# Where VectorE's sums of a weight matrix stand in a fused attention and ELU kernel: program order, halves, and the order of four copies

## Chip, cores, metric

One core of a Trainium2 chip. The metric is the device time of one execution in microseconds (us). The program runs on one core.

## The reference, cut to what matters

```python
x = attn(x, state)          # (8 batches, 544 tokens, 512): token rows and state rows
h = x @ w_in                # 4352 x 512 @ 512 x 2048
g = where(h > 0, h, exp(min(h, 0)) - 1)
out = g @ w_out             # 4352 x 2048 @ 2048 x 512, fp32
```

The kernel works batch by batch. Per batch there is a first product (**FFN1**: 16 rows of h, transposed, 128 x 512 each, two matmuls a row, which a trace shows as four records, then ELU) and a second product. Batch 0 forms the second product plainly, while the weights are still arriving. From batch 1 on it is a seven-product (Strassen) scheme, which needs sums of quarters of w_out; VectorE forms these once, about the time when batch 1 begins.

## The kernel before

Cuts are marked with `...`. A bank is a part of PSUM, the memory that TensorE's matmuls write their results to; in this kernel a bank is written again only after another engine has read its result out. m is the weight matrix of one batch's FFN1, made on TensorE in PSUM and copied out into m_sb. An instruction issued through `vector` keeps its program order relative to the others so issued while `vector.on` is true; afterwards a scheduler places it.

```python
class InOrder:
    ...
            ins = getattr(self.engine, name)(*args, **kw)
            return tc.keep_in_program_order(ins) if self.on else ins

def ffn1(b, fo):                       # row fo of FFN1
    ps = bank(4 + fo % 2 if b == 0 else 3 + (fo + 1) % 3)   # banks 4, 5, 3, 4, 5, 3 ...
    for k in range(G):                 # two matmuls
        matmul(ps, m_t[b, fo // 4][:, k, fo % 4 * P : (fo % 4 + 1) * P], st[b, k, "aT"], ...)
    return ps

def weight_sum(i):                     # two sums of 128x1024 each
    ...
    x, y = {1: (b12, b11), 2: (b22, t_w.get(1)), 3: (b22, b12), 4: (b21, t_w.get(2))}[i]
    combine(t_w[i], x, y)              # combine: vector.tensor_tensor, subtract

def first_batch():
    ...                                # o_ps: banks 0 to 3, batch 0's result
    for i in range(2):
        o_sb = opool.tile([P, 2, DM], FP32, tag="o", name="o_sb")
        for c in range(2):
            (scalar.copy, vector.tensor_copy)[c](out=o_sb[:, c], in_=o_ps[2 * i + c])
        store(0, i, o_sb)

def batch(b):
    for fo in range(FO):               # FO = 16
        elu(ffn1(b, fo), fo)           # 2 operations on ScalarE, 1 on VectorE into g_all
        if fo == FO // 4 + 1:          # after row 5: m for rows 8 to 15
            for c in (2, 3):
                make_m(b, c, first=6 if c == 2 else 0)
        if FO // 4 + 1 <= fo < FO // 4 + 5:
            c, g = divmod(fo - FO // 4 - 1, G)
            copy_m(b, 2 + c, g, vector.tensor_copy)
        if b == 1 and fo % 4 == 3:
            weight_sum((1, 2, 4, 3)[fo // 4])
        ...
    ...
    if b == 1:                         # second level: sums of sums, into spare parts of w_in and others
        hooks += [lambda: second[4].weights(t_w[4]), lambda: second[3].weights(b22)]
        hooks += [lambda: second[5].weights(t_w[1]), lambda: second[7].weights(t_w[3])]
    ...

first_batch()
load_x(2, [sync])
for e in (vector, scalar, gpsimd):
    e.on = False
for b in range(1, B):
    batch(b)
```

So `weight_sum` stands in batch 1's loop, but VectorE was released before that loop, and the scheduler moved all eight sums to the front. Two of the four copies of batch 0's result are VectorE's: banks 1 and 3. FFN1's row 2 writes bank 3.

Of the kernel before, what the change touches and what calls it, by code (L numbers as in the profile page):

```python
# [25 lines left out]
def kernel(  # L26
# [67 lines left out]
    class InOrder:  # L94
# [10 lines left out]
    tensor, sync, vector, scalar, gpsimd = (  # L105
        InOrder(e) for e in (nc.tensor, nc.sync, nc.vector, nc.scalar, nc.gpsimd)
    )
# [25 lines left out]
    def load_x(b, engines):  # L133
        x_t[b] = xpool.tile([P, R, DM], FP32, name="x_sb")
        x_v = x[b].rearrange("h (p r) d -> p r h d", r=R)
        for r in range(R):
            engines[r % len(engines)].dma_start(
                out=x_t[b][:, r].rearrange("p (h d) -> p h d", d=D), in_=x_v[:, r]
            )
# [213 lines left out]
    def fetch_w_in(c, k):  # L353

        for i in range(2):
            sync.dma_start(
                out=w_in[:, 2 * (k + i) : 2 * (k + i) + 2],
                in_=w_in_mem[:, 2 * (c + i) : 2 * (c + i) + 2],
            )

    def make_m(b, c, h=None, first=6):

        c_in = c if b < 2 else c % 2
        halves = slice(2 * c_in, 2 * c_in + 2) if h is None else slice(2 * c_in + h, 2 * c_in + h + 1)
        assert h is None or b == 0
        st[b, "m", c] = by_state(b, [w_in[:, halves, m] for m in range(NP)], first)

    def copy_m(b, c, g, copy):
        if g == 0:
            m_t[b, c] = mpool.tile([P, G, 512], FP32, name="m_sb")  # L370
        copy(out=m_t[b, c][:, g], in_=st[b, "m", c][:, g])
# [20 lines left out]
    def elu(ps, fo):  # L392

        max_part(fo, exp_part(ps), ps)

    def ffn1(b, fo):


        ps = bank(4 + fo % 2 if b == 0 else 3 + (fo + 1) % 3)
        for k in range(G):  # L400
            matmul(
                ps,
                m_t[b, fo // 4][:, k, fo % 4 * P : (fo % 4 + 1) * P],
                st[b, k, "aT"],
                start=(k == 0),
                stop=(k == G - 1),
            )
        return ps
# [28 lines left out]
    def combine(out, x, y, op=ALU.subtract):  # L437
        for o, i, j in zip(out, x, y):
            vector.tensor_tensor(out=o, in0=i, in1=j, op=op)
# [3 lines left out]
    b11, b12, b21, b22 = (halves(w_k[:, :, e, h]) for e in range(2) for h in range(2))  # L443
    t_w = {3: b12}

    def weight_sum(i):

        if i != 3:
            t_w[i] = [
                work.tile([P, FO // 4, DM // 2], FP32, tag="w", name="t_w") for k in range(2)  # L450
            ]
        x, y = {1: (b12, b11), 2: (b22, t_w.get(1)), 3: (b22, b12), 4: (b21, t_w.get(2))}[i]
        combine(t_w[i], x, y)

    class Second:

# [194 lines left out]
    def attention(b):  # L651


        def both(*fs):
            for g in range(G):
                for f in fs:
                    f(b, g)

        def s0():

            for i in range(2):
                turn_x(b, i, 4 + 2 * i)
            for i in range(2):
                copy_x(b, i)

        def s1():

            scores(b)
            for c in range(2):
                make_m(b, c, first=4 - 2 * c)  # L670
            both(column_max, turn_scores, column_exp, row_max, row_subtract, row_exp)
            both(row_sum, row_scale, column_total)
            for c in range(2):
                for g in range(G):
                    copy_m(b, c, g, (scalar.copy, vector.tensor_copy)[g])

        def s2():
            turn_state(b)
            copy_state(b)
            both(turn_tokens)  # L680

        nop = lambda: None
        return [s0, s1, nop, nop, s2, lambda: (state_read(b), keep_read(b))]

    def store(b, i, o_sb):
        rows = out_b[b, 0:S].rearrange("(p r) c -> p r c", r=R)
        sync.dma_start(out=rows[:, 2 * i : 2 * i + 2], in_=o_sb)

    def first_batch():
# [30 lines left out]
        w, h, e = [], {}, {}  # L720
# [61 lines left out]
                        copy_m(*num, g, scalar.copy)  # L782
        for g in range(G):
            copy_m(1, 1, g, scalar.copy)
        for i in range(2):
            o_sb = opool.tile([P, 2, DM], FP32, tag="o", name="o_sb")
            for c in range(2):
                (scalar.copy, vector.tensor_copy)[c](out=o_sb[:, c], in_=o_ps[2 * i + c])
            store(0, i, o_sb)

    def batch(b):
        for fo in range(FO):
            elu(ffn1(b, fo), fo)
            if fo == FO // 4 + 1:
                for c in (2, 3):
                    make_m(b, c, first=6 if c == 2 else 0)
            if FO // 4 + 1 <= fo < FO // 4 + 5:
                c, g = divmod(fo - FO // 4 - 1, G)
                copy_m(b, 2 + c, g, vector.tensor_copy)
            if b == 1 and fo % 4 == 3:  # L800
                weight_sum((1, 2, 4, 3)[fo // 4])
            if b > 1 and fo == FO // 4 + 2:
                fetch_w_in(0, 0)
        nxt = b + 1 < B
        hooks = attention(b + 1) if nxt else [turn_read]
        if nxt and b > 0:
            s1 = hooks[1]
            hooks[1] = lambda: (s1(), fetch_w_in(2, 0))
        if b + 2 < B:
            hooks += [lambda: load_x(b + 2, [sync])]  # L810
        if b == 1:
            hooks += [lambda: second[4].weights(t_w[4]), lambda: second[3].weights(b22)]
            hooks += [lambda: second[5].weights(t_w[1]), lambda: second[7].weights(t_w[3])]
            used = {k: second[k] for k in (4, 3)}
        else:
            used = second
        whole = Strassen(2, used)
        whole.sums()
        for f in whole.steps():
            f()  # L820
            if hooks:
                hooks.pop(0)()
        if not nxt:
            fetch_w_in(2, 2)
        for i in (1, 0):
            store(b, i, whole.o_sb[i])

    def states():
# [8 lines left out]
        for b in range(B):  # L837
# [3 lines left out]
            )  # L841

    first_batch()
    load_x(2, [sync])
    for e in (vector, scalar, gpsimd):
        e.on = False
    for b in range(1, B):
        batch(b)
# [31 lines left out]
```

## Time and profile before

| | before |
|---|---|
| median of 3 runs | 763.11 us (762.99 to 763.88) |
| span of the profiled run | 761.6 us |
| TensorE busy, share of the chain that ended last | 96%, 90% |
| FFN1 of batch 1, first matmul to the next product | 32.75 us |
| FFN1 of batch 2, the same | 29.54 us |

How to read it: TensorE is the bound, and in batch 1's first product it stands still for 3.2 us that batch 2 does not lose. The lines are in the prediction below.

### The profile page before, as it was taken

To read this page: it belongs to the slowest core of one execution; us is meant where nothing else is said; L and a number is where in the kernel's file an instruction comes from. 1 tells how busy PE (TensorE), PEld (TensorE's weight loads), DVE (VectorE), ACT (ScalarE), POOL (GpSimd) and SP (SyncE) were. 2 spreads that over 40 slices of the span, in tenths; PEclk is the share of its full clock that TensorE was granted. 3 is DMA by queue.
4 is the path that set the end of the run, shared out by engine and by line. 5 is a ranking of instruction groups with operands and counts; after the bars stand their busy time and mean duration, and the time that the engine had idled before them with its cause. 6 is when DMAs were issued, how large, how long until landed. Compare 5 with 4: busy or idle time off the path is not lost.

```text
span 761.6 us, 11358 instructions
## 1 busy us (share of the span) xinstructions
PE 730.9 (96%) x4640; PEld 505.2 (66%) x4640; DVE 467.3 (61%) x855; ACT 312.3 (41%) x575; POOL 35.2 (5%) x38
## 2 busy tenths in 40 slices
PE   3699999899999999999999999999999999999996
PEld 1334444367964798468946795579746994699885
DVE  2999989758336674667555763667456745566330
ACT  4799874553036311642055303631265206410420
POOL 0200002002000200001000200020001100000000
PEclk9999999999999999999999999999999999999999
DMA  9656900402212221313030221222122003003001
GB/s 281 221 194 215 316 16 1 111 1 111 56 56 111 112 56 56 111 57 110 29 138 1 111 57 64 102 111 57 56 110 87 26 29 137 1 1 139 28 1 28
DMA packets 49172, 66.79 MB, mean 88 GB/s; under 512 B 36832, under 2 KB 36832, under 8 KB 45280
## 3 DMA queue, kind: packets, MB, share of 16 engines
q1 hardware_dynamic: 45952, 65.28, 25.5%
q10 hardware_dynamic: 3168, 0.79, 0.5%
q8 instruction: 36, 0.59, 0.3%
q14 instruction: 16, 0.13, 0.1%
HBM read 52.95 MB, written 13.11 MB: 87 GB/s over the span
## 4 chain that ended last, share of the span: by engine, by line
PE 90%; DVE 6%; ACT 1%; DMA 1%; issue 0%; ACTq 0%; DVEq 0%
PE ps L100 90%; DVE t_w L100 1%; DVE w_in L100 1%; DMA x_sb<-in_x_dram 1%; DVE total_t L100 1%; DVE s L100 0%; DVE g_all L100 0%; DVE w_out L100 0%; DMA s_sb<-in_state_dram 0%; ACT raw L100 0%; DVE top L100 0%; ACT e_sb L100 0%; DVE aT L100 0%; DVE m_sb L100 0%; DVE top_t L100 0%; DVE o_sb L100 0%
## 5 line engine op out<-in xcount | busy, mean ns | idle before, releaser
L100 PE MATMUL ps<-w_out,g_all 128*128 128x256 f32 (+2 forms) x1088 | 234.7, 367 | 0.7
L100 PE MATMUL ps<-aT,m_sb 128*128 128x512 f32 x512 | 228.7, 600 | 6.2 <-DVE aT L100 2.5
L100 PEld LDWEIGHTS ps<-w_out,g_all 128*128 128x128 f32 x1088 | 175.6, 191 | 54.4 <-issue 36.0
L100 PEld LDWEIGHTS ps<-aT,m_sb 128*128 128x128 f32 x512 | 96.1, 191 | 129.1 <-issue 116.7
L100 ACT ACTIVATE e_sb<-ps 128x512 f32<-128x512 f32 (+1 forms) x144 | 82.5, 573 | 224.0 <-PE ps L100 206.3
L100 DVE SCALAR_TENSOR_TENSOR g_all<-e_sb,ps 128x512 f32<-128x512 f32 (+1 forms) x144 | 94.4, 657 | 116.3 <-ACT e_sb L100 116.3
L100 DVE TENSOR_TENSOR o_sb<-o_sb,ps 128x128 f32<-128x128 f32 (+2 forms) x170 | 52.7, 310 | 76.1 <-PE ps L100 74.4
L100 PE MATMUL ps<-t_w,s 128*128 128x256 f32 (+1 forms) x480 | 89.3, 338 | 0.0
L100 ACT ACTIVATE e_sb<-e_sb 128x512 f32<-128x512 f32 (+1 forms) x144 | 87.3, 606 | 4.6
L100 PEld LDWEIGHTS ps<-t_w,s 128*128 128x128 f32 x480 | 77.1, 191 | 7.3 <-DVE o_sb L100 0.2
L100 ACT COPY o_sb<-ps 128x512 f32<-128x512 f32 (+2 forms) x52 | 21.3, 424 | 121.8 <-PE ps L100 114.7
L100 ACT ACTIVATE raw<-raw 128x512 f32<-128x512 uint32 x64 | 43.5, 680 | 1.0
L100 POOL TENSOR_TENSOR t_sb<-t_sb,top_t 128x512 f32<-128x512 f32 x16 | 17.7, 1110 | 533.3 <-DVE top_t L100 533.3
L100 DVE TENSOR_TENSOR s<-s,g_all 128x512 f32<-128x512 f32 (+1 forms) x36 | 32.1, 896 | 14.4 <-PE ps L100 14.2
L100 DVE TENSOR_TENSOR g_all<-g_all,s 128x512 f32<-128x512 f32 (+1 forms) x36 | 31.9, 886 | 9.6 <-PE ps L100 9.6
L100 PE MATMUL ps<-w_in,kT 64*32 64x512 f32 (+1 forms) x576 | 33.6, 554 | 0.0
L100 DVE TENSOR_TENSOR g_all<-g_all 128x512 f32<-128x512 f32 (+1 forms) x36 | 32.2, 895 | 0.5
L100 PE MATMUL ps<-t_w,g_all 128*128 128x128 f32 (+1 forms) x240 | 32.1, 282 | 0.0
L100 DVE TENSOR_TENSOR s<-g_all 128x512 f32<-128x512 f32 (+1 forms) x36 | 31.6, 895 | 0.5
L100 PE MATMUL ps<-w_in,s 128*128 128x128 f32 x240 | 30.7, 275 | 0.0
L100 PEld LDWEIGHTS ps<-t_w,g_all 128*128 128x128 f32 x240 | 29.8, 192 | 0.5
L100 DVE TENSOR_REDUCE top<-ps 128x1 f32<-128x512 f32 x16 | 11.0, 685 | 29.1 <-PE ps L100 29.1
(78 smaller groups left out, 578.5 us busy)
## 6 DMA issues: line engine op xcount, KB each, us to landing
w_in<-w_in_mem SPq DMA_DIRECT2D x26, 1024.0 KB, 6.1
raw<-in_moe_w_in_dram SPq DMA_DIRECT2D x16, 512.0 KB, 5.9
raw<-in_moe_w_out_dram SPq DMA_DIRECT2D x16, 512.0 KB, 3.3
out_dram<-o_sb SPq DMA_DIRECT2D x16, 512.0 KB, 2.6
x_sb<-in_x_dram SPq DMA_DIRECT2D x30, 256.0 KB, 4.5
w_in_mem<-w_in SPq DMA_DIRECT2D x4, 1024.0 KB, 6.4
x_sb<-in_x_dram ACTq DMA_DIRECT2D x2, 256.0 KB, 6.4
out_dram<-o_sb SPq DMA_DIRECT2D x8, 64.0 KB, 1.7
```

Of the source, the lines that this page charges most:

```text
L100: ins = getattr(self.engine, name)(*args, **kw)
```

## The change

Intent: keep VectorE in program order up to the end of batch 1's FFN1, so that the sums stay where the program writes them, in pieces of one half after every second row; and copy batch 0's last bank first, since FFN1 needs that bank first.

```diff
-    def weight_sum(i):
-
-        if i != 3:
+    def weight_sum(i, half):
+
+        if i != 3 and half == 0:
             t_w[i] = [
                 work.tile([P, FO // 4, DM // 2], FP32, tag="w", name="t_w") for k in range(2)
             ]
         x, y = {1: (b12, b11), 2: (b22, t_w.get(1)), 3: (b22, b12), 4: (b21, t_w.get(2))}[i]
-        combine(t_w[i], x, y)
+        k = slice(half, half + 1)
+        combine(t_w[i][k], x[k], y[k])
@@ first_batch
-        for i in range(2):
+
+        for i in (1, 0):
             o_sb = opool.tile([P, 2, DM], FP32, tag="o", name="o_sb")
-            for c in range(2):
+            for c in (1, 0):
                 (scalar.copy, vector.tensor_copy)[c](out=o_sb[:, c], in_=o_ps[2 * i + c])
@@ batch
-            if b == 1 and fo % 4 == 3:
-                weight_sum((1, 2, 4, 3)[fo // 4])
+            if b == 1 and fo % 2 == 1:
+                weight_sum((1, 2, 4, 3)[fo // 4], fo % 4 // 2)
             if b > 1 and fo == FO // 4 + 2:
                 fetch_w_in(0, 0)
+        vector.on = False
@@ end
-    for e in (vector, scalar, gpsimd):
+    for e in (scalar, gpsimd):
         e.on = False
```

## The prediction

> **What bounds the kernel now.** I read the page first (busy shares, chain), then the chain of waits in order of time, then TensorE's timeline where the chain leaves TensorE, and last a table of two stretches that do the same work.
>
> ```profile
> span 761.6 us, 11358 instructions
> PE 730.9 (96%) x4640; PEld 505.2 (66%) x4640; DVE 467.3 (61%) x855; ACT 312.3 (41%) x575; POOL 35.2 (5%) x38
> PE 90%; DVE 6%; ACT 1%; DMA 1%; issue 0%; ACTq 0%; DVEq 0%
> ```
>
> TensorE is busy 96% of the span and is 90% of the chain that ended last. Nothing in the diff touches a matmul (the order of instructions on TensorE and on ScalarE is the same in both kernels), so the change can win only time in which TensorE now stands still in the part it reorders: the sums of w_out and the first product of batch 1 (call it FFN1: 16 rows of two matmuls each). The chain in order of time shows VectorE in it there:
>
> ```profile
> 130.48 0.62 DVE aT L100
> 131.10 1.11 DVE w_out L100
> 132.21 0.60 DVE t L100
> 132.81 0.60 DVE w_out L100
> 133.41 0.60 DVE o_sb L100
> 134.01 0.60 DVE t L100
> 134.61 0.60 DVE t_w L100
> 135.21 0.61 DVE o_sb L100
> 135.82 0.04 issue
> 135.87 7.15 PE ps L100 x16
> ```
>
> Two copies of batch 0's result (o_sb) stand behind sums that nobody needs yet. Row 2 of FFN1 writes PSUM bank 3, which holds batch 0's last result until the second of these copies ends. TensorE's timeline shows what that costs:
>
> ```profile
> 130.46 3.60 PE L100 MATMUL ps<-aT,m_sb 128*128 128x512 f32 x8
> 135.87 7.13 PE L100 MATMUL ps<-aT,m_sb 128*128 128x512 f32 x16 [1.81 <-DVE o_sb L100]
> 142.93 1.95 PE L100 MATMUL ps<-w_in,kT 64*32 64x512 f32 x32
> 144.81 5.42 PE L100 MATMUL ps<-aT,m_sb 128*128 128x512 f32 x12
> 150.47 1.98 PE L100 MATMUL ps<-aT,m_sb 128*128 128x512 f32 x4 [0.24 <-DVE g_all L100]
> 152.81 10.57 PE L100 MATMUL ps<-aT,m_sb 128*128 128x512 f32 x24 [0.35 <-DVE g_all L100]
> ```
>
> FFN1 of batch 1 runs from 130.46 to 163.21, where the next product starts. The same work in batch 2 runs from 216.64 to 246.18 without a wait:
>
> ```profile
> 130.46:163.21 32.75, 30.35 (x97) 12.30 (x96) 23.55 (x37) 18.40 (x30) 0.00 (x0) 1.00 0.27 64
> 216.64:246.18 29.54, 29.54 (x98) 12.57 (x97) 14.82 (x22) 18.39 (x30) 0.00 (x0) 1.00 0.23 89
> ```
>
> (columns: stretch, length, busy TensorE, weight loads, VectorE, ScalarE, GpSimd, granted clock, DMA share, GB/s.) So **3.2 us**, 32.75 less 29.54, is all that can be won here: 0.4% of 763. Starts tell it better than the idle column, because the modelled ends hide the tail: eight records take 8 x 0.43 = 3.44 us, so row 2 could start at 133.90 and started at 135.87 (1.97 us); row 9 should start at 144.81 + 3 x 1.72 = 149.97 and starts at 150.47 (0.50); row 10 loses 0.62. Sum 3.09.
>
> **What the Trainium skill says.** "PSUM — Partial Sum Buffer", section "PSUM bank collisions raise a hardware error", says that an access to a bank by TensorE must be guarded against another engine still reading it; so the copy out of bank 3 is a real dependency. The trace agrees: TensorE's 1.81 us wait is for o_sb. "VectorE: DVE Perf Modes", section "Why `tensor_tensor` can't do 2×_2P or 4×", says that an fp32 sum of two tensors gets no faster mode; its errata section gives (N+151)/0.96 ns, 1224 ns at 1024 columns. The trace agrees (1225 ns for the sums of g_all), so splitting a sum in two makes it no cheaper. "SBUF — State Buffer" says, where it sums up the shared port pair, that a VectorE operation with two SBUF inputs contends with GpSimd. The w_out sums of before that lie beside GpSimd's work are indeed longer (two of t_w<-w_out at a mean of 1820 ns), and from 130.46 on GpSimd has no work, so the moved sums should take 1.22.
>
> **The change part by part.** VectorE's order in the changed kernel, against before: (a) the eight 1024-wide sums and the small ones after them leave the stretch from 117 to 136, where VectorE was full; (b) the two o_sb copies follow right after the two transposes of aT, bank 3 first; (c) the halves of sums come one after every second row of FFN1; (d) three sums into w_in (left to the scheduler, as their release from program order is not in the loop) land between the first and the second copy of m_sb; (e) some 7 us of sums move behind the last row. No instruction is added or removed in work: about the same sums, other places.
>
> (a) and (b): VectorE is free from about 122.5 (attention without sums between), waits for the last matmul of batch 0 to end, about 130.6, and copies bank 3 by 131.3. Row 2 can start at 133.90. This wins **1.97 us** with 2.6 us to spare. The earlier aT is worth nothing: TensorE has no gap from 107 to 134.
>
> (c) and (d), worked through with durations of the trace. TensorE: 1.72 us a row; 1.88 us for the m products after row 5. A row's result is ready for VectorE 3.20 us after the row's start (batch 2: 216.64 to 219.84). VectorE back to back: 0.60 for 512 columns (144.93, two copies, 146.13), 1.14 for 1024 (150.93 to 152.07), 0.71 for one that needs the one before it (two in 1.42 at 108.93). Rows start at 130.46, 132.18, 133.90, 135.62, 137.34, 139.06; m products at 140.78; rows 6, 7, 8 at 142.66, 144.38, 146.10. VectorE: row 0 at 133.66, row 1 135.38, sum 135.98, row 2 137.12, row 3 138.82, sum 139.42, row 4 140.56, row 5 142.26; up to here nothing is late, since a bank is used again three rows later. Then m copy 142.86, sum 143.46, three dependent w_in sums 144.60, 145.31, 146.02, row 6 146.62, second m copy 147.22 to 147.90. The second matmul of row 8 needs that copy and would start at 146.96; it starts near 147.95. **A new wait of 1.0 us**, on m_sb. From there: row 9 at 148.81, 10 at 150.53, 11 at 152.25 (its bank is read out by row 8's operation, 151.30 to 151.99: 0.2 us to spare), 12 at 153.97, 15 at 159.13, end 160.85. The rest fits: each two rows of 3.44 us hold 2 x 0.60 + 1.14 + at most 0.60. The old waits of 0.50 and 0.62 at rows 9 and 10 are gone. Batch 2's stretch is 0.14 longer than the sum of its rows, so the end is 161.0 against 163.21: **2.2 us won** of 3.2.
>
> (e): after the last row (VectorE about 162.9) some 7.2 us remain: two 1024 sums of g_all and s and one of w_out at 1.14, six small ones at 0.60 to 0.71. They end near 170.3. The next attention's maximum needs VectorE at 172.84 - 2.2 = 170.6: just in time; and its first reader on TensorE in before is at 184.76, several us behind the exponentials, so a few tenths late cost nothing. From there on TensorE's order and the rest of VectorE's are those of before, and the gain should stay as a rigid shift to the end.
>
> Sum: 763.11 - 2.2 = **760.9 us**.
>
> **The rivals.** (1) No new wait, all 3.2 us won: 759.9. For it: VectorE is busy only 23.55 of 32.75 us in this stretch before. Against it: the order puts 4.0 us of sums and row 6 between the two m copies. It would hold if VectorE ran these a good deal quicker than I assumed. (2) VectorE becomes the bound of FFN1: between row 0 and row 15 I count 16 x 0.60 + 4 x 0.60 + 9 x 1.14 + 5 x 0.66 = 25.6 us of work in 29 us. If operations cost 0.1 more than assumed (a wait on another engine ahead of most of them), the wait at row 8 grows to 1.5, row 11 becomes late too, and 1 us or less is won: 762.1 to 762.6. For it: before lost 1.1 us at rows 9 and 10 to the same crowding. (3) The time moves to later waits: the sums behind row 15 delay the attention of batch 2 and what is won comes back at 172 to 190. Then 762 to 763. Against it: the 5 us and more between the exponentials and the first matmul that needs them. (4) The wait for bank 3 was put down wrongly and something else (the store) holds row 2: nothing won. Against it: the matmul starts 0.05 us after that copy ends.
>
> **Range and chances.** The middle is 2.2 won; three runs of before spread by 0.9 us, which is as large as my doubt about the new wait. I take 760.0 to 762.1. Two per cent would be 15 us, five times all that VectorE costs in this stretch, and nothing in the change touches the other batches: faster 0.005, within 0.99, slower 0.005.
>
> **What would show it.** Right: in the changed profile row 2 starts 3.44 us after row 0 with no wait on o_sb; TensorE has one wait of about 1 us in FFN1, at row 8, put down to m_sb (or whatever VectorE did just before it); FFN1 lasts 30.6 us; the next product starts 2.2 us earlier and so does every later batch. Wrong: the first gap still there (rival 4), waits of over 0.3 us at other rows, on g_all (rival 2), no wait on m_sb (rival 1), or a gap after 165 that before had not (rival 3).

## The result, and the profile after

| | before | changed |
|---|---|---|
| median of 6 runs | 763.35 us (762.99 to 764.20) | 761.43 us (760.76 to 763.84) |
| ratio, 95% interval | | 0.9978 (0.9963 to 0.9992) |
| FFN1 of batch 1 | 32.75 us | 30.56 us |
| start of batch 1's FFN1 to start of batch 2's | 86.18 us | 83.98 us |

A ratio is the mean time of one kernel's runs over the mean of the other's runs of the same rounds, so it is not quite the ratio of the medians quoted here. The change is a gain of 0.2%. A second set of five runs of the changed kernel gave 0.9974 (0.9961 to 0.9987).

The page of the changed kernel:

```profile
span 759.8 us, 11359 instructions
PE 729.6 (96%) x4640; PEld 504.6 (66%) x4640; DVE 465.9 (61%) x855; ACT 312.1 (41%) x575; POOL 34.1 (4%) x38
PE 93%; DVE 3%; DMA 1%; ACT 1%; issue 0%; ACTq 0%; DVEq 0%
```

VectorE's share of the chain that ended last fell from 6% to 3%. The chain in order of time no longer enters VectorE near 117, only at 142 (start, length, what):

```profile
142.53 0.69 DVE g_all L100
143.22 0.60 DVE m_sb L100
143.81 1.13 DVE t_w L100
144.94 0.62 DVE w_in L100
...
145.65 0.70 DVE w_in L100
...
146.38 0.69 DVE w_in L100
147.07 0.60 DVE g_all L100
147.66 0.61 DVE m_sb L100
148.28 0.04 issue
148.32 41.76 PE ps L100 x285
```

This is the one new wait: row 5's ELU, first m copy, one half sum, three sums into w_in, row 6's ELU, second m copy, and only then row 8's second matmul. TensorE's timeline has it as its only gap in FFN1:

```profile
130.74 10.46 PE L100 MATMUL ps<-aT,m_sb 128*128 128x512 f32 x24
141.13 1.95 PE L100 MATMUL ps<-w_in,kT 64*32 64x512 f32 x32
143.01 4.56 PE L100 MATMUL ps<-aT,m_sb 128*128 128x512 f32 x10
148.32 13.14 PE L100 MATMUL ps<-aT,m_sb 128*128 128x512 f32 x30 [0.76 <-DVE m_sb L100]
161.30 3.62 PE L100 MATMUL ps<-w_out,g_all 128*128 128x256 f32 x16
```

The first six rows are now one piece of 24 records: the wait on o_sb is gone. Ten records after 143.01 should end their issue at 143.01 + 10 x 0.43 = 147.31; the next starts at 148.32, so the wait costs 1.01 us (the 0.76 of the line counts from a modelled end); by lengths it is 30.56 less batch 2's 29.54, 1.02. On VectorE the two copies come as soon as batch 0's last matmuls are done, after idle time that before was filled with sums, and the next attention's maximum starts right behind the backlog:

```profile
122.61 0.71 DVE L100 STREAM_TRANSPOSE aT<-t_sb 128x512 f32<-128x512 f32 x1 [0.65 <-POOL t_sb L100]
130.94 1.29 DVE L100 COPY o_sb<-ps 128x512 f32<-128x512 f32 x2 [7.62 <-PE ps L100]
...
170.93 0.69 DVE L100 TENSOR_REDUCE top<-ps 128x1 f32<-128x512 f32 x1 [0.18 <-PE ps L100]
```

VectorE stands idle for 7.62 us before the copies, and 0.18 us before the maximum: the backlog fits to within two tenths. From the start of batch 2's FFN1 to the end the two traces are alike within 0.2 us.

The spans differ by 1.8 us and not by 2.2 because the profiled run of the changed kernel began FFN1 at 130.74 and not at 130.46. In all thirteen traces FFN1 of batch 1 begins 90.9 us after TensorE's second group of batch 0's rows, which starts between 39.06 and 40.00; the whole spread of FFN1's start (129.96 to 130.89) is made in the first 40 us, which no edit here touches. Hence the measure in the experiments is a length, FFN1 or start to start, and not the time.

### The profile page after: what moved, and what is told of

It reads as the page before. It is cut to its first block, busy times and chain, and to the rows that moved or that the text cites. A ratio compares the mean times of both kernels' runs of the same rounds, so it can differ in the third digit from the quotient of the medians.

```text
span 759.8 us, 11359 instructions
## 1 busy us (share of the span) xinstructions
PE 729.6 (96%) x4640; PEld 504.6 (66%) x4640; DVE 465.9 (61%) x855; ACT 312.1 (41%) x575; POOL 34.1 (4%) x38
## 4 chain that ended last, share of the span: by engine, by line
PE 93%; DVE 3%; DMA 1%; ACT 1%; issue 0%; ACTq 0%; DVEq 0%
PE ps L100 93%; DVE w_in L100 1%; DMA x_sb<-in_x_dram 1%; DVE s L100 0%; DMA s_sb<-in_state_dram 0%; ACT raw L100 0%; DVE total_t L100 0%; ACT e_sb L100 0%; ACT xT L100 0%; DVE top L100 0%; DVE g_all L100 0%; DVE aT L100 0%; DVE t_sb L100 0%; DVE m_sb L100 0%; DVE top_t L100 0%
## 5 line engine op out<-in xcount | busy, mean ns | idle before, releaser
L100 PEld LDWEIGHTS ps<-w_in,s 128*128 128x128 f32 x240 | 28.7, 192 | 0.1
```

## The experiments

My theory: the gain is the wait for bank 3 and two smaller waits (rows 9 and 10), won because the copies and ELU operations no longer stand behind sums; 1 us is given back at row 8, because VectorE does 4 us of other things between the two m copies. The main rivals: that VectorE's whole load bounds FFN1, so that moving one thing only moves the wait; that the copy order or the halves are what wins; and that the time comes back later.

| run | edit | FFN1, us | start to start, us | time, us (runs) |
|---|---|---|---|---|
| before | | 32.75 | 86.18 | 763.35 (6) |
| changed | | 30.56 | 83.98 | 761.43 (6) |
| e1_free | VectorE released early again | 32.73 | 86.16 | 762.98 (1) |
| e2_actcopy | before, all four copies on ScalarE | 31.02 | 84.45 | 761.84 (1) |
| e3_oldcopy | copies in the old order | 30.57 | 83.99 | 761.72 (1) |
| e4_whole | whole sums in program order | 30.87 | 84.29 | 761.52 (1) |
| e5_double | one half sum twice between the m copies | 31.51 | 84.93 | 762.95 (1) |
| e6_kept | sums into w_in kept in order | 29.91 | 84.44 | 762.10 (1) |
| e7_both | both m copies together | 30.99 | 84.41 | 761.41 (1) |
| e8_kept_both | both of these | 29.80 | 84.32 | 761.73 (1) |
| e9_after | changed kernel again | 30.57 | 84.00 | 761.65 (5) |
| e10_early | sums in VectorE's idle time | 29.91 | 83.33 | 760.85 (5) |
| e11_early_both | that, and both m copies together | 29.55 | 82.97 | 760.64 (5) |

All were correct. The single times carry the 0.9 us of the first 40 us; read the lengths.

### e1_free: without program order

```diff
-        vector.on = False
@@ end
-    for e in (scalar, gpsimd):
+    for e in (vector, scalar, gpsimd):
```

> The changed kernel with VectorE released from program order where the kernel before released it (half sums and the new copy order stay). FFN1 of batch 1 is counted from its first matmul to the start of the next product: 32.75 us before, 30.56 us changed. My theory (what wins is that the copies out of banks 3 and 1 no longer stand behind sums): the scheduler puts the sums ahead of the copies again, row 2 waits for the copy of bank 3 about 1.9 us, rows 9 and 10 wait again, FFN1 is 32.6 to 32.8 us, total as before. Rival (the half sums or the copy order win it): FFN1 near 30.6 us.

FFN1 was 32.73 us, as before. TensorE's timeline of this run has before's three waits, to the hundredth:

```profile
129.96 3.60 PE L100 MATMUL ps<-aT,m_sb 128*128 128x512 f32 x8
135.36 7.13 PE L100 MATMUL ps<-aT,m_sb 128*128 128x512 f32 x16 [1.81 <-DVE o_sb L100]
...
149.96 1.98 PE L100 MATMUL ps<-aT,m_sb 128*128 128x512 f32 x4 [0.24 <-DVE g_all L100]
152.29 10.57 PE L100 MATMUL ps<-aT,m_sb 128*128 128x512 f32 x24 [0.35 <-DVE g_all L100]
```

So halves and copy order alone win nothing: the scheduler puts the sums ahead of the copies here too. Program order is the part that works.

### e2_actcopy: the copies off VectorE, sums where they were

```diff
-                (scalar.copy, vector.tensor_copy)[c](out=o_sb[:, c], in_=o_ps[2 * i + c])
+                scalar.copy(out=o_sb[:, c], in_=o_ps[2 * i + c])
```

(in the kernel before.)

> The kernel before with all four copies of batch 0's result on ScalarE instead of two on VectorE; the sums stay where they were. My theory: bank 3 is free at about 1 us after batch 0's last matmul, row 2 starts 3.44 us after row 0 with no wait; row 3 may wait 0.2 us, since VectorE reaches row 0 only after its sums; the waits at rows 9 and 10 (0.5 and 0.6 us) stay; FFN1 about 30.9 us. Rival (the store or something else than VectorE's copy holds row 2): the wait of 1.8 us stays, 32.7 us.

FFN1 was 31.02 us. Its first six rows are one piece again:

```profile
130.57 10.82 PE L100 MATMUL ps<-aT,m_sb 128*128 128x512 f32 x24
```

The wait for bank 3 is gone, the waits at rows 9 and 10 stay (148.85 with 0.24 idle ahead of it, 151.19 with 0.35). So this wait of before was VectorE's late copy and not the store or a transfer, and it is worth 32.75 - 31.02 = 1.73 us by itself; I had it at 1.97, less 0.2 for row 3, which waits for a late ELU operation (the first 24 records take 10.82 us here and 10.46 in the changed kernel, so that cost 0.36). This one-line edit takes most of what the change takes.

### e3_oldcopy: the order of the copies

```diff
-        for i in (1, 0):
+        for i in range(2):
             ...
-            for c in (1, 0):
+            for c in range(2):
```

(in the changed kernel.)

> The changed kernel with the copies in the old order (bank 3 last of VectorE's two, not first). My theory: bank 3 is then free 0.6 us later, about 1.5 us after batch 0's last matmul, and row 2 needs it only 3.3 us after that matmul: no wait, FFN1 30.56 us as changed, so the order of copies is worth nothing here. Rival (the order of copies is what wins): row 2 waits, FFN1 above 31.

FFN1 was 30.57 us against 30.56. Once the sums are out of the way, bank 3 is ready early enough in either order. This part of the change is worth nothing here.

### e4_whole: whole sums

```diff
-            if b == 1 and fo % 2 == 1:
-                weight_sum((1, 2, 4, 3)[fo // 4], fo % 4 // 2)
+            if b == 1 and fo % 4 == 3:
+                for half in range(2):
+                    weight_sum((1, 2, 4, 3)[fo // 4], half)
```

> The changed kernel with the sums of w_out whole again, both halves after every fourth row, still in program order. My theory, by the same walk as in the prediction: the wait at row 8 shrinks to about 0.2 us, because one half sum no longer stands between the m copies, but a wait of about 0.95 us comes at row 11, whose bank is held by row 8's operation behind two sums; FFN1 30.7 to 30.8 us, so halves are worth 0.2 us at most. Rival (halves are needed): two sums in a row delay several rows, FFN1 31.5 us or more.

FFN1 was 30.87 us: halves are worth 0.31 us, a little more than the 0.2 that I allowed. The waits are where the walk put them: the trace has one put down to g_all, ahead of row 11 (0.64 us idle by the modelled end, some 0.9 by starts), and the rest, about 0.35 where I had 0.2, lies inside the run of records before it, at row 8.

### e5_double: more work between the m copies

```diff
                 weight_sum((1, 2, 4, 3)[fo // 4], fo % 4 // 2)
+                if fo == FO // 4 + 1:
+                    combine(t_w[2][:1], b22[:1], t_w[1][:1])
```

> The changed kernel with the half sum between the two m copies done twice (one more 1024-wide sum, 1.14 us back to back, same result). My theory (row 8 waits for the second m copy, which waits for what VectorE does between the copies): the wait at row 8 grows from 1.0 to 2.1 us, no other row is late, FFN1 31.7 us. Rival (VectorE has slack there and the wait is the attention's or a transfer's): FFN1 stays near 30.6.

FFN1 was 31.51 us, 0.95 more than the changed kernel for 1.14 us of added work. Row 8 waits longer on the same tile, and nothing else is late:

```profile
149.42 13.14 PE L100 MATMUL ps<-aT,m_sb 128*128 128x512 f32 x30 [1.71 <-DVE m_sb L100]
```

The scheduler put the doubled sum between the first and second of the three dependent sums into w_in, where it filled the time that the second had waited for the first, so it cost a little less than 1.14. The wait at row 8 is a chain on VectorE, without slack.

### e6_kept, e7_both, e8_kept_both: the two ways to shorten that chain

```diff
+            def kept(k, w):
+                vector.on = True
+                second[k].weights(w)
+                vector.on = False
+
-            hooks += [lambda: second[5].weights(t_w[1]), lambda: second[7].weights(t_w[3])]
+            hooks += [lambda: kept(5, t_w[1]), lambda: kept(7, t_w[3])]
```

(e6 and e8)

> The changed kernel with the six sums into w_in kept in program order too, so that they leave FFN1 for the second products. My theory: 2.1 us less stands between the m copies, but the second copy is still behind row 6's operation, which waits for ScalarE: the wait at row 8 shrinks from 1.0 to about 0.2 us, FFN1 29.8 us. Where the sums go, between the additions to the result near 40 to 55 us after FFN1 began, TensorE may wait up to 0.8 us in all. Rival (the second copy of m is not what counts): FFN1 stays near 30.6.

```diff
-            if FO // 4 + 1 <= fo < FO // 4 + 5:
+            if b == 1 and fo in (FO // 4 + 1, FO // 4 + 3):
+                for g in range(G):
+                    copy_m(b, 2 + (fo - FO // 4 - 1) // 2, g, vector.tensor_copy)
+            if b > 1 and FO // 4 + 1 <= fo < FO // 4 + 5:
```

(e7 and e8)

> The changed kernel with both halves of an m copied together (after rows 5 and 7), ahead of the sums. If only the place of the second copy counts, row 8 no longer waits and FFN1 is 29.6 us. If VectorE as a whole is the bound there (the prediction's second rival), the sums merely delay other rows: by my walk row 9 by 0.1 and row 11 by 1.2 us, FFN1 30.85 us, no better than the changed kernel. I expect the second.

> Both of the two edits before together: sums into w_in out of FFN1, and both m copies ahead of the half sum. By my walk no row is late: FFN1 29.55 us, the length that batch 2 has. Later, as in the run with the sums kept, TensorE may wait up to 0.8 us at the additions to the result.

Results: e6's FFN1 29.91 us, e7's 30.99, e8's 29.80. For e8 I had expected 29.55 and no late row, which was wrong: the 40 records after the m products take 17.69 us against 17.43 in batch 2, and the late one is row 11's first, again behind row 8's ELU. Taking 2.1 us of sums out of FFN1 (e6) removes most of the wait. Merely letting the second m copy pass the sums (e7) does not: the wait moves to row 11, whose bank row 8's ELU holds. TensorE's timeline in e7:

```profile
142.42 9.09 PE L100 MATMUL ps<-aT,m_sb 128*128 128x512 f32 x20
152.46 8.85 PE L100 MATMUL ps<-aT,m_sb 128*128 128x512 f32 x20 [0.95 <-DVE g_all L100]
```

So between rows 6 and 11 VectorE's load as a whole is the bound, and the second m copy is only where it showed first; that e11 below makes the same two copies early with less load and has no wait fits this. This is the prediction's second rival, in a milder form than I gave it: true for five rows and not for all of FFN1.

But e6 and e8 lose in all: start to start they are 84.44 and 84.32 us against 83.98. The sums kept in order now fall into the second product, where VectorE must empty a PSUM bank every 0.9 us, and TensorE waits there (timeline of e6):

```profile
212.48 1.16 PE L100 MATMUL ps<-b,s 128*128 128x128 f32 x8 [0.84 <-DVE o_sb L100]
```

By starts, 212.48 - 210.58 = 1.90 us for a product that otherwise takes 0.89, a loss of 1.0; I had allowed for up to 0.8. Here time moved to a later wait, as the third rival says; the changed kernel itself shows none there.

### e9_after, e10_early, e11_early_both: the idle time ahead of the copies

e10 moves the six half sums that don't write w_out to the start of the 7.6 us in which the changed kernel's VectorE has nothing to do (with four small sums they take longer than that, and push the copies back); the last, in-place sum stays late in FFN1. e11 adds e7's edit.

```diff
@@ first_batch, after the plan
+        for i in (1, 2, 4):
+            for half in range(2):
+                weight_sum(i, half)
         for i in (1, 0):
@@ batch
-            if b == 1 and fo % 2 == 1:
-                weight_sum((1, 2, 4, 3)[fo // 4], fo % 4 // 2)
+            if b == 1 and fo in (FO - 3, FO - 1):
+                weight_sum(3, fo // 2 % 2)
```

> The changed kernel again, unchanged, beside the next two on one chip: FFN1 30.56 us, 2.2 us from FFN1's start to batch 2's less than before (84.0 against 86.2), total about 2 us below before, with the spread of the first 50 us of the program (0.5 us) on top.

> The changed kernel with the six half sums that read w_out only put into VectorE's idle time between the transposes of aT and the copies (7.6 us without work there), so that none stands in FFN1 but the last, in-place one. My theory: six sums of 1.14 and four small ones end about 9.2 us after the transposes, bank 3 is read out 1 us before row 2 needs it, row 8 waits 0.2 us for the second m copy (behind the three sums into w_in and row 6), FFN1 29.7 to 29.9 us, start to start 83.2, total 0.8 us below the changed kernel. Rival (sums ahead of the copies always cost the wait for bank 3): row 2 waits, FFN1 31 us or more.

> The same with both halves of an m copied together. Now VectorE has room in FFN1, so unlike in the run with that edit alone no row should be late: FFN1 29.6 us as in batch 2, start to start 83.0, total 1.0 us below the changed kernel and 3.1 below before. Rival (VectorE is still the bound): a wait at row 9 or 11 as in the run with both copies together alone, FFN1 30.5 or more.

FFN1 was 30.57, 29.91 and 29.55 us: e11's is as long as batch 2's, and the ten rows after the m products run in one piece (first line). VectorE's timeline in e11 shows the sums, back to back, and the copies behind them:

```profile
143.12 17.43 PE L100 MATMUL ps<-aT,m_sb 128*128 128x512 f32 x40
...
123.37 2.32 DVE L100 TENSOR_TENSOR t_w<-w_out 128x1024 f32<-128x1024 f32 x2
125.60 4.62 DVE L100 TENSOR_TENSOR t_w<-w_out,t_w 128x1024 f32<-128x1024 f32 x4
...
132.68 1.28 DVE L100 COPY o_sb<-ps 128x512 f32<-128x512 f32 x2
```

FFN1 begins at 130.85 in that run, so row 2 is due at 134.29, and bank 3 is read out by 133.4. So sums ahead of the copies do not always cost a wait: here they begin after GpSimd's last operation and take 1.16 us each (2.32 for two), where before's were longer (see part (a) below). The edit that won nothing alone (e7) is worth 0.36 us here, since VectorE now has room. On one chip, five runs each: e9 761.65, e10 760.85, e11 760.64 us (760.32 to 760.85). The ratio of e11 to before is 0.9960 (0.9946 to 0.9974), against 0.9974 for the changed kernel. e11 has the shortest length, with the 3.2 us that could be won here won in full (86.18 - 82.97 = 3.21, one trace each); no run of it overlaps one of e9 (761.26 to 761.86), but its times do overlap e10's (760.17 to 761.14), so what sets these two apart is the length and not the time.

## Why the prediction was right, point by point

- **What could be won.** 3.2 us, from batch 2's FFN1. e11 won 3.21. Right.
- **Parts (a) and (b), the copies behind sums: 1.97 us.** The first six rows run in one piece in the changed kernel, with no wait on o_sb. e2 isolates the dependency and e1 shows that without program order the wait returns whole. Right; and within (b), the phrase "bank 3 first" carried no weight: e3 puts it at nothing, which the prediction's 2.6 us to spare implied and did not say. One cost was overlooked: four of the eight sums of before overlap GpSimd's operations and are lengthened (the last section has the numbers), in all by 2.3 us. VectorE's timeline has no idle time from 117.10 to the copy of bank 3, which ends at 135.81; 2.3 us less would put that end near 133.5 (an estimate), before row 2 was due at 133.90. How much of the wait is the sums' place and how much their lengthening is not shown: the change removes both, and no run separates them.
- **Parts (c) and (d), the new wait: 1.0 us at row 8, on m_sb.** 1.01 by starts, on m_sb, and the only one in FFN1. e5 confirms the chain. Right, and in the last tenth by luck: the prediction reads "two in 1.42" as 0.71 from one dependent sum to the next, but 1.42 is a start-to-start time plus one duration; the three sums started 0.79 and 0.73 us apart (144.86, 145.65, 146.38). So the second m copy ended 17.53 us after FFN1's start and not 17.44; TensorE reached row 6 0.07 us late as well (12.27 against 12.20), and the two nearly cancel. The reason given was narrower than the truth: e7 shows that the m copy is not alone, and that the load behind it would hold row 11 as much.
- **Part (e), 7.2 us of backlog that ends just in time.** The backlog took 7.35 us (163.40 to 170.75). The maximum waits 0.18 us for TensorE and none for VectorE; no later wait in the changed kernel. Right.
- **Rivals.** The first (no wait) fell; the fourth (something else holds row 2) fell with e2; the third does not hold for the change but does for e6 and e8; the second holds for rows 6 to 11.
- **The sum.** 2.2 us predicted and 2.20 start to start. The median fell from 763.35 to 761.43, by 1.9; 760.9 was half a microsecond too low. Of this, 0.24 is the median of before, which I took from three runs (763.11; six gave 763.35); the rest lies within the 0.9 us by which the first 40 us spread.

## What to carry to other kernels

Ahead of the bound engine's first use of a buffer, look at what stands in the emptying engine's queue in front of the copy: work that nobody needs yet, put there by a scheduler, can cost more than its own time suggests. But holding all such work back to its program place also leaves that engine idle earlier and crowded later; the best version here began the sums in a measured idle stretch, left the copies behind them, and checked the due time of the one bank that mattered. When an edit only moves a wait (e7), try it again after the load has been taken away (e11).

## What the Trainium skill lacked or had wrong

- "VectorE: DVE Perf Modes", section "The DRAIN you can't avoid", says that a semaphore between two operations costs nothing extra, which it measured with copies. Here it does not hold for sums that need the result of the one before: they start 0.73 us apart (changed kernel: 145.65, 146.38), while independent operations of the same 512 columns start 0.60 us apart though each lasts 0.68 (143.13, 143.73). The dependence costs 0.13 us, for which no page has a figure.
- "SBUF — State Buffer", section "Who interferes with whom", says that a VectorE operation with two SBUF inputs contends with a GpSimd operation that reads SBUF, and gives no time for this pair. These runs have one. Four of before's 1024-column sums overlap GpSimd's operations on t_sb and take 1.70, 1.94, 1.81 and 1.77 us; in the changed kernel none does. The group of the first two is, before and changed,

```profile
L100 DVE TENSOR_TENSOR t_w<-w_out 128x1024 f32<-128x1024 f32 x2 | 3.6, 1820 | 0.0
```

```profile
L100 DVE TENSOR_TENSOR t_w<-w_out 128x1024 f32<-128x1024 f32 x2 | 2.4, 1218 | 0.0
```

  and the means of the other two groups are 1360 ns (four sums) and 1476 ns (two) before, 1214 and 1216 changed: 2.3 us in all. GpSimd's first two operations take 3.03 us together before and 2.05 us after. The page is right on this pair: two of the four sums end 1.08 and 1.07 us after the GpSimd operation that they overlap (126.83 after 125.75, 130.47 after 129.40), nearly a whole sum later.
- No page was found that says how far the start of a whole program spreads from run to run: here TensorE reaches the same point between 39.06 and 40.00 us in thirteen traces, which was nearly half of the gain to be measured. Its granted clock in the first 40 us was 0.91 in five of them and 1.00 in eight, but the two groups overlap in that start, so the cause stays open.
